# One more product summed into a PSUM bank, attention's first batch moved ahead of the weights, and products started while weights are still split

## The chip, the cores and the metric

One Trainium2 chip, one of its cores. The metric is the device time of one execution in microseconds (us); the median of three runs counts. A change of 0.2% of it is about 3 us.

## The reference, cut to what matters

```python
def _attn_ref(q, k, v, g_norm):              # q, k, v: (8, 8, 576, 64)
    kv = np.einsum('bhsd,bhse->bhde', k, v)
    out = np.einsum('bhsd,bhde->bhse', q, kv)
    rms = np.sqrt(np.mean(out * out, axis=-1, keepdims=True) + 1e-06)
    return (out / rms * g_norm).astype(np.float32)
...
x = attn_out.transpose(0, 2, 1, 3).reshape(4608, 512)
h = x @ w_in;   g = np.maximum(0.01 * h, h);  x = g @ w_out      # 512 -> 2048 -> 512
h = x @ w2_in;  g = h - np.tanh(h);           out = g @ w2_out   # 512 -> 2048 -> 512
```

The matrices have 4608 rows; the weights come as 8-byte floating point and are turned into 4-byte numbers on the chip.

## The kernel before, in words

Four matrix multiplications follow each other: "up 1" (512 to 2048, eight superblocks of 576 rows), "down 1" (2048 to 512), "up 2" (nine superblocks of 512 rows) and "down 2". Each is done with Winograd's form of Strassen's scheme: operands are cut in 2 by 2 blocks, sums of blocks (S on the left, T on the right) are formed, and seven products P1 to P7 are summed into four result blocks "11", "21", "12", "22". Every operand is kept as a high and a low 16-bit part, so that a product over one 128-deep slice is three matmuls (`three`, L490).

In up 1 and up 2 a unit of work is one of eight 128-column strips i of one superblock: seven products of six matmuls each. The matmuls of P1, P6 and P7 add up in one PSUM bank "a"; after each of these, ScalarE copies the running sum out (`keep`, L526 and L528), as c1, u2 and u3. P2 has bank "b", P4 bank "d", P5 and then P3 bank "c". VectorE adds such a bank to one of the copies (`add`, L537), which gives a result block in `g`: "11" from P2 and c1, "21" from u3 minus P4, "22" from P5 and u3, "12" from P3 on top of P5 and u2. A product that goes on in a bank waits until the copy or add before it has read the bank. TensorE's order inside a round is the table `ORDER`, with a lag in units. When "12" is there, ScalarE applies the activation (up 1, L1004) or ScalarE, VectorE and GpSimd do (up 2, L1151 and L1154), and the unit goes to DRAM.

Nothing is scheduled by the compiler: the class `Plan` keeps planned times for ScalarE ("A"), VectorE ("V") and GpSimd ("G") and one running time for TensorE (`plan.pe`), and emits every instruction in the order of its planned time. On the chip each engine takes its instructions in that order and waits at each for what it needs. `fit` looks for the first gap on an engine in which a job fits, and lets it overlap the next job by `OVER`.

The opening. q, k, v of batch 0 come in four pairs of heads (`load_pair`), between the weights of up 1, which come in 16 units of 512 KB (`convert`, n = 0): 3 units behind each of the four pairs, then the last 4. A unit is turned into 4-byte numbers by one ScalarE and four VectorE instructions (L315 to L338). After all 16 a scale is worked out (L254 to L269), and then `split_first` writes the high and low parts of the strips: ScalarE (L363) and VectorE (L366) each for three and four blocks, and GpSimd forms four differences (L373) in between. Attention (`pair`: pk, pq, po, pm) of a pair is some 36 fp32 matmuls with ScalarE copies between them; a batch's end is `norms`: a root, three reciprocals, a trip through DRAM (iv, bc), a GpSimd multiplication (xg, L879), four GpSimd sums (L469) and the high and low parts (L430, L437). Batch 1's four pairs are planned ahead of START, the planned time of the first product; the pairs of batches 2 to 7 are slipped between products of up 1 (`between1`). SyncE issues every DMA.

While up 1 runs, the weights of down 1 and then of up 2 are converted and split with the same instructions; those of down 2 during up 2.

Of the kernel before, what the change touches and what calls it, by code (L numbers as in the profile page):

```python
# [17 lines left out]
DRAM = bass.MemoryType.DRAM  # L18

# [9 lines left out]
NOP = 7  # L29
P = 128  # L30
# [13 lines left out]
class Plan:  # L44
# [5 lines left out]
    HAND, OVER = 0.25, 0.35  # L50
# [27 lines left out]
    def chain(self, t, steps):  # L78
# [3 lines left out]
        def go(k, t):  # L82
# [4 lines left out]
            for eng, dur, fn in some:  # L87
                t_ = t if eng is None else self.fit(eng, t, dur, min(self.OVER, dur / 3))
# [42 lines left out]
def body(ctx, tc, q, k, v, g_norm, w1, w2, w3, w4, out):  # L131
# [13 lines left out]
    NL, NM, NX = 22, 11, 8  # L145
# [149 lines left out]
    def convert(n, i, kk, t, land, keep=None):  # L295
# [50 lines left out]
        def store():  # L346
# [4 lines left out]
        steps = [(None, land, load), ("A", 0.7, one), ("V", 0.78, two), ("V", 0.45, shift), ("V", 0.7, low),  # L351
                 ("V", 0.7, high)]
        plan.chain(t, steps + ([(None, 0.0, store)] if keep is None else []))

    def right_stages(w, dst, scale):
# [15 lines left out]
        def less(o, a, b):  # L371
# [7 lines left out]
            ("G", 0.5, lambda: less(t2, b22, t1)), ("G", 0.5, lambda: less(t4, t2, b21)),  # L379
# [3 lines left out]
    def split_late(n, i, kk, t, place):  # L383

        held = {}

        def load():
            need(("wf", n, i, kk))
            need(f"s_w{n + 1}")
            held["u"] = place.take([P, NU], F32, "unit")  # L390
            nc.sync.dma_start(out=held["u"].ap, in_=wf[n, i, kk])
# [4 lines left out]
        def store():  # L396
            done_.add(("wd", n, i, kk))
            nc.sync.dma_start(out=wd[n, i][:, kk], in_=held["o"].ap.rearrange("p a b c -> p (a b c)"))
            place.give(held["u"])
# [3 lines left out]
        stages = right_stages(lambda: held["u"].ap, lambda: held["o"].ap, lambda: small[f"s_{name}"])  # L403
# [94 lines left out]
    class Blocks:  # L498

        def __init__(self, banks, width, place, scale=None, minus=None, ready=None):
            self.banks, self.n, self.place, self.ready = banks, width, place, ready
            self.scale = scale
            self.minus = -scale if isinstance(scale, float) else minus
            self.t, self.ps, self.done = {}, {}, set()
# [4 lines left out]
        def bank(self, p):  # L511
            which = BANK_OF[p]
            need = {6: "c1", 7: "u2", 3: "22"}.get(p)
            assert need is None or need in self.done, ("planned too late", plan.now, need)
            if p in (1, 2, 4, 5):
                self.ps[which] = bank(self.banks[which], f"ps_{which}")
            return self.ps[which][:, :self.n], p in (1, 2, 4, 5)

        def keep(self, nm):
            self.done.add(nm)  # L520
            self.t[nm] = X.take([P, self.n], F32, nm)
            src, t = self.ps["a"][:, :self.n], self.t[nm].ap
# [6 lines left out]
            if nm == "u3":  # L529
# [21 lines left out]
        def after(self, p, e):  # L551

            t, f = e + 0.15, self.n / 1000.0
            if p == 4:
                return e
            if p in (1, 6, 7):
                name = {1: "c1", 6: "u2", 7: "u3"}[p]
                end = plan.do("A", t, f + 0.15, lambda: self.keep(name))
                if p == 7:
                    self.u3 = end + 0.2  # L560
                    plan.do("V", self.u3, 1.2 * f + 0.14, lambda: self.add("21", "d", "u3", sub=True))
                return end
            blk, which, name = {2: ("11", "b", "c1"), 5: ("22", "c", "u3"), 3: ("12", "c", "u2")}[p]
            if p == 5:
                t = max(t, self.u3)
            return plan.do("V", t, 1.2 * f + 0.14, lambda: self.add(blk, which, name, last=True))

        u3 = 0.0
# [5 lines left out]

# [675 lines left out]
```

## Time and profile before

| | |
|---|---|
| median of 3 runs | 1580.79 us (1579.94 to 1581.8) |
| the profiled execution, its own time | 1581.95 us |
| its span in the profile | 1580.1 us |
| TensorE matmul busy | 1468.2 us (93%) |
| VectorE, ScalarE, GpSimd busy | 1311.1 us (83%), 864.4 us (55%), 749.4 us (47%) |
| mean granted TensorE clock | 0.972 |

The span runs from the first to the last instruction in the trace; 1.85 us of the execution lie around it. Matmuls are pipelined, so a busy TensorE may be one that goes on slowly. ps_a to ps_d are the banks of the products, PE is TensorE, DVE VectorE, ACT ScalarE, POOL GpSimd and SP SyncE. The granted clock 1.00 is 2.4 GHz, 0.50 is 1.2 GHz.

### The profile page before, as it was taken

What the parts mean: (1) busy time and instruction counts of PE and PEld (TensorE: products, weight loads), DVE (VectorE), ACT (ScalarE), POOL (GpSimd) and SP (SyncE); (2) the same over time, 40 slices, a digit from 0 to 9 for tenths busy, and PEclk for the clock granted to TensorE, in tenths of its full rate; (3) what the DMA queues carried; (4) which work ended last, traced back from release to release, by engine and by line L of the source; (5) the groups of instructions that cost most, each with busy time, mean ns of one, the idle gap of its engine ahead of it and who ended that gap; (6) DMA issues with size and microseconds to landing.
All of it is one profiled execution on the core that took longest, in us unless ns stands there. A gap on an engine that the chain in (4) does not pass through costs nothing. (4 is left out here: it accounts for less than half of the span.)

```text
span 1580.1 us, 33070 instructions
## 1 busy us (share of the span) xinstructions
PE 1468.2 (93%) x12658; PEld 1197.5 (76%) x12658; DVE 1311.1 (83%) x2113; ACT 864.4 (55%) x1381; POOL 749.4 (47%) x758
## 2 busy tenths in 40 slices
PE   5289998999899999999999899999999999999998
PEld 3157776766677777777777688878888888888887
DVE  5876777868777899899997799998999998888881
ACT  3367665656665745454453366656776655445450
POOL 0375311334533446667664244446886654444440
PEclk7589999999999999999999999999999999999999
DMA  9636887889966954555554855645668844444431
GB/s 223 193 96 182 268 272 245 267 267 298 296 248 216 375 197 162 176 171 192 168 180 153 295 194 194 210 158 197 222 244 311 306 126 144 136 138 151 139 120 34
DMA packets 190527, 322.59 MB, mean 204 GB/s; under 512 B 55712, under 2 KB 133024, under 8 KB 190368
## 3 DMA queue, kind: packets, MB, share of 16 engines
q1 hardware_dynamic: 190368, 320.48, 61.7%
q8 instruction: 99, 1.62, 0.4%
q14 instruction: 60, 0.49, 0.1%
HBM read 190.84 MB, written 129.56 MB: 203 GB/s over the span
## 5 line engine op out<-in xcount | busy, mean ns | idle before, releaser
L490 PEld LDWEIGHTS <-w 128*128 128x128 f16 x8400 | 819.4, 98 | 234.8 <-issue 58.3
L469 POOL TENSOR_TENSOR gl<-gl 128x256 f32<-128x256 f32 (+1 forms) x272 | 308.2, 1135 | 302.6 <-DVE gl L469 86.1
L490 PE MATMUL ps_c<-ops,w 128*128 128x288 f16 (+1 forms) x2400 | 331.7, 282 | 27.0 <-DVE g L537 26.8
L490 PE MATMUL ps_a<-ops,w 128*128 128x288 f16 (+1 forms) x2400 | 331.8, 283 | 7.5 <-ACT u L524 3.1
L373 POOL TENSOR_TENSOR unit<-unit 128x128 f32<-128x128 f32 x192 | 136.5, 715 | 109.3 <-DVE wo L366 78.0
L490 PEld LDWEIGHTS <-ops 128*128 128x128 f16 x1728 | 169.0, 98 | 24.9 <-issue 5.4
L490 PE MATMUL ps_b<-opa,w 128*128 128x288 f16 (+1 forms) x1200 | 174.7, 283 | 0.0
L490 PE MATMUL ps_d<-opa,w 128*128 128x288 f16 (+1 forms) x1200 | 173.0, 281 | 0.6 <-DVE g L537 0.5
L490 PE MATMUL ps_a<-opa,w 128*128 128x288 f16 (+1 forms) x1200 | 166.3, 282 | 5.2 <-DVE opa L437 2.6
L469 DVE TENSOR_TENSOR gl<-gl 128x256 f32<-128x256 f32 (+1 forms) x272 | 161.9, 601 | 3.7
L432 ACT ACTIVATE ops<-gl,inv 128x1024 f16<-128x1024 f32 x72 | 82.5, 1146 | 133.9 <-POOL gl L469 133.9
L1154 POOL TENSOR_TENSOR g<-g,th 128x512 f32<-128x512 f32 x72 | 101.1, 1406 | 95.9 <-ACT th L1151 95.3
L879 POOL TENSOR_TENSOR xg<-xg,bc 128x1152 f32<-128x1152 f32 x16 | 42.8, 2681 | 206.1 <-DMA bc<-iv 135.6
L490 PEld LDWEIGHTS <-opa 128*128 128x128 f16 x1296 | 127.6, 99 | 15.6 <-DVE opa L439 0.2
L439 DVE SCALAR_TENSOR_TENSOR ops<-gl,inv,ops 128x1024 f16<-128x1024 f32 x72 | 105.7, 1469 | 31.3 <-ACT ops L432 31.3
L430 ACT ACTIVATE ops<-gl 128x1152 f16<-128x1152 f32 x64 | 74.2, 1161 | 94.8 <-POOL gl L469 94.8
L437 DVE TENSOR_TENSOR ops<-gl,ops 128x1152 f16<-128x1152 f32 x64 | 97.9, 1530 | 7.4 <-ACT ops L430 7.2
L490 PE MATMUL ps_a<-w,ops 128*128 128x256 f16 x864 | 97.2, 273 | 3.4 <-ACT u L528 2.8
L490 PE MATMUL ps_c<-w,ops 128*128 128x256 f16 x864 | 97.3, 273 | 0.2 <-DVE osb L537 0.2
L528 ACT ACTIVATE u<-ps_a,up 128x256 f32<-128x256 f32 x144 | 68.2, 473 | 49.2 <-PE ps_a L490 43.8
L469 POOL TENSOR_TENSOR x1g<-x1g 128x256 f32<-128x256 f32 x72 | 65.7, 916 | 53.9 <-DVE opa L439 25.0
L537 DVE SCALAR_TENSOR_TENSOR g<-ps_c,u 128x288 f32<-128x288 f32 x128 | 57.7, 451 | 39.2 <-PE ps_c L490 39.1
(118 smaller groups left out, 2203.6 us busy)
## 6 DMA issues: line engine op xcount, KB each, us to landing
g<-g SPq DMA_DIRECT2D x64, 576.0 KB, 4.9
gl<-g SPq DMA_DIRECT2D x64, 576.0 KB, 4.9
g<-g SPq DMA_DIRECT2D x72, 512.0 KB, 3.3
gl<-g SPq DMA_DIRECT2D x72, 512.0 KB, 4.5
wd<-wo SPq DMA_DIRECT2D x48, 448.0 KB, 3.3
w<-wd SPq DMA_DIRECT2D x24, 896.0 KB, 6.9
words<-in_moe_w_in_dram SPq DMA_DIRECT2D x64, 256.0 KB, 5.2
words<-in_moe_w_out_dram SPq DMA_DIRECT2D x64, 256.0 KB, 4.3
```

Source lines behind the costliest of these rows:

```text
L373: nc.gpsimd.tensor_tensor(out=o, in0=a, in1=b, op=ALU.subtract)
L430: nc.scalar.activation(out=o, in_=i_, func=AF.Copy)
L432: nc.scalar.activation(out=o, in_=i_, func=AF.Identity, scale=scale())
L437: nc.vector.tensor_tensor(out=o, in0=i_, in1=h, op=ALU.subtract)
L439: nc.vector.scalar_tensor_tensor(out=o, in0=i_, scalar=scale(), in1=h, op0=ALU.mult, op1=ALU.subtract)
L469: lambda: e.tensor_tensor(out=g()[:, o], in0=g()[:, a], in1=g()[:, b], op=op),
L490: nc.tensor.matmul(out=out_, lhsT=a, rhs=c, start=start and m == 0, stop=stop and m == n - 1, skip_group_check=not fresh,)
L528: nc.scalar.activation(out=t, in_=src, func=AF.Identity, scale=self.scale)
L537: nc.vector.scalar_tensor_tensor(out=o, in0=src, scalar=self.minus if sub else self.scale, in1=t, op0=ALU.mult, op1=ALU.add,)
L879: nc.gpsimd.tensor_tensor(out=x, in0=x, in1=held[kk].ap, op=ALU.mult)
L1154: e.tensor_tensor(out=g()[:, n], in0=g()[:, n], in1=held["t"].ap[:, n], op=ALU.subtract)
```

## The change

Four things are changed, three of them in the two up stages' scheduling.

- P4 in up 1 and up 2: the right-hand sum T4 is formed with the other sign (`minus4`, for the weights n = 0 and 2), and P4 adds up in bank "a" behind P1, P6 and P7. ScalarE copies the sum straight into `g` as block "21". Bank "d" is not used there; bank "a" is taken from three banks in turn. The VectorE add of "21" is not issued. The order within a round is new (`ORDER1`, `ORDER2`); in up 2 P3 runs two units behind instead of one.
- The opening: one weight unit behind each of batch 0's pairs instead of three, then the other 12. The copies of po into xg for batch 0 go from VectorE to ScalarE. START is `last + 45` instead of `last + 58`. Three of batch 1's pairs are planned ahead of START, the fourth five products behind it; batches 2 and 3 begin later.
- The splits of up 1's strips are planned 4.2 us apart instead of 5.0, and may run three strips ahead of the buffers instead of two.
- The plan's costs: ScalarE jobs may overlap by 0.6 (0.35 before), all by half of their length (a third before); conversion jobs are planned somewhat differently. One slot more in pool M, one less in L; up 2's units for splitting come from M.

The diff, with unchanged lines cut:

```diff
@@ -47,7 +48,7 @@
-    HAND, OVER = 0.25, 0.35
+    HAND, OVER = 0.25, {"A": 0.6, "V": 0.35, "G": 0.35}
     def __init__(self):
@@ -85,7 +86,7 @@
-                t_ = t if eng is None else self.fit(eng, t, dur, min(self.OVER, dur / 3))
+                t_ = t if eng is None else self.fit(eng, t, dur, min(self.OVER[eng], dur / 2))
                 def run(fn=fn):
@@ -142,7 +143,7 @@
-    NL, NM, NX = 22, 11, 8
+    NL, NM, NX = 21, 12, 8
@@ -348,11 +349,12 @@
-        steps = [(None, land, load), ("A", 0.7, one), ("V", 0.78, two), ("V", 0.45, shift), ("V", 0.7, low),
-                 ("V", 0.7, high)]
+        slow = 1.0 if keep else 1.1
+        steps = [(None, land, load), ("A", 0.7, one), ("V", 0.72 * slow, two), ("V", 0.4 * slow, shift),
+                 ("V", 0.63 * slow, low), ("V", 0.63 * slow, high)]
-    def right_stages(w, dst, scale):
+    def right_stages(w, dst, scale, minus4):
@@ -376,18 +378,20 @@
-            ("G", 0.5, lambda: less(t2, b22, t1)), ("G", 0.5, lambda: less(t4, t2, b21)),
+            ("G", 0.5, lambda: less(t2, b22, t1)),
+            ("G", 0.5, (lambda: less(t4, b21, t2)) if minus4 else (lambda: less(t4, t2, b21))),
-    def split_late(n, i, kk, t, place):
+    def split_late(n, i, kk, t, place, place_u=None):
+        place_u = place_u or place
         def load():
-            held["u"] = place.take([P, NU], F32, "unit")
+            held["u"] = place_u.take([P, NU], F32, "unit")
         def room():
@@ -396,11 +400,11 @@
         def store():
-            place.give(held["u"])
+            place_u.give(held["u"])
-        stages = right_stages(lambda: held["u"].ap, lambda: held["o"].ap, lambda: small[f"s_{name}"])
+        stages = right_stages(lambda: held["u"].ap, lambda: held["o"].ap, lambda: small[f"s_{name}"], n == 2)
@@ -499,34 +503,41 @@
         def __init__(self, banks, width, place, scale=None, minus=None, ready=None):
+            self.one4 = "d" not in banks
-            self.t, self.ps, self.done = {}, {}, set()
+            self.t, self.ps, self.done, self.kept = {}, {}, set(), {}
         def scaled(self, scale, minus):
         def bank(self, p):
-            which = BANK_OF[p]
-            need = {6: "c1", 7: "u2", 3: "22"}.get(p)
+            which = "a" if p == 4 and self.one4 else BANK_OF[p]
+            need = {6: "c1", 7: "u2", 3: "22", 4: "u3" if self.one4 else None}.get(p)
-            if p in (1, 2, 4, 5):
+            start = p in (1, 2, 5) or p == 4 and not self.one4
+            if start:
-            return self.ps[which][:, :self.n], p in (1, 2, 4, 5)
+            return self.ps[which][:, :self.n], start
         def keep(self, nm):
-            self.t[nm] = X.take([P, self.n], F32, nm)
-            src, t = self.ps["a"][:, :self.n], self.t[nm].ap
+            if nm == "21":
+                t = self.place(nm)
+            else:
+                self.t[nm] = X.take([P, self.n], F32, nm)
+                t = self.t[nm].ap
+            src = self.ps["a"][:, :self.n]
-            if nm == "u3":
+            if nm == ("21" if self.one4 else "u3"):
         def add(self, blk, which, nm, sub=False, last=False):
@@ -551,30 +562,24 @@
         def after(self, p, e):
-            if p == 4:
+            if p == 4 and not self.one4:
-            if p in (1, 6, 7):
-                name = {1: "c1", 6: "u2", 7: "u3"}[p]
+            if p in (1, 6, 7, 4):
+                name = {1: "c1", 6: "u2", 7: "u3", 4: "21"}[p]
-                if p == 7:
-                    self.u3 = end + 0.2
-                    plan.do("V", self.u3, 1.2 * f + 0.14, lambda: self.add("21", "d", "u3", sub=True))
+                self.kept[name] = end + 0.2
+                if p == 7 and not self.one4:
+                    plan.do("V", self.kept[name], 1.2 * f + 0.14, lambda: self.add("21", "d", "u3", sub=True))
-            if p == 5:
-                t = max(t, self.u3)
+            t = max(t, self.kept[name])
-        u3 = 0.0
     def mm(T):
-    ORDER = ((2, 0), (6, 0), (4, 0), (3, 1), (1, -1), (7, 0), (5, 0))
-    def up(blk, T, NS, xops, act, scale, banks, between, freed):
+    def up(blk, T, NS, xops, act, scale, banks, order, between, freed):
@@ -618,17 +620,24 @@
-        for n in range(-1, N + 1):
-            for p, lag in ORDER:
+        def place(m):
+            def get(b):
+                if m not in g:
+                    g[m] = L.take([P, 4, T], F32, "g")
+                return g[m].ap[:, BLOCKS.index(b)]
+            return get
+        for n in range(-1, N + 2):
+            for p, lag in order:
-                if n == N:
-                    plan.pe += 1.4
-                if n == 0 and p in (6, 7):
+                if m == 0 and p in (6, 7) or m == N - 1 and p == 4:
+                if blk == 0 and m < NP and p == 1:
+                    plan.pe += SLOW
-                    bk[m] = Blocks(banks(m), T, None, None if callable(scale) else scale)
+                    bk[m] = Blocks(banks(m), T, place(m), None if callable(scale) else scale)
@@ -818,11 +827,18 @@
             def copy():
-                nc.vector.tensor_copy(out=xg[b, kk].ap[:, 2 * n + r], in_=po[r][:, :T1])
+                o_ = xg[b, kk].ap[:, 2 * n + r]
+                if b == 0:
+                    nc.scalar.activation(out=o_, in_=po[r][:, :T1], func=AF.Copy)
+                else:
+                    nc.vector.tensor_copy(out=o_, in_=po[r][:, :T1])
-            plan.do("V", end, 0.46, copy)
+            if b == 0:
+                plan.do("A", end, 0.42, copy)
+            else:
+                plan.do("V", end, 0.46, copy)
         def m():
@@ -905,8 +921,8 @@
     def place_w1(i, kk):
         def get():
-                if i < NP - 2:
-                    kept[i] = Held(wpool.tile([P, 2 * NU], F32, tag=f"w{i + 2}", name=f"w1f{i}"), None)
+                if i < NP - 3:
+                    kept[i] = Held(wpool.tile([P, 2 * NU], F32, tag=f"w{i + 3}", name=f"w1f{i}"), None)
@@ -917,8 +933,8 @@
-        order += [("w",) + u for u in UNITS[3 * hp:3 * hp + 3]]
-    order += [("w",) + u for u in UNITS[12:]]
+        order += [("w",) + u for u in UNITS[hp:hp + 1]]
+    order += [("w",) + u for u in UNITS[4:]]
@@ -932,11 +948,11 @@
     def split_first(i, kk):
-            lambda: kept[i].ap[:, NU * kk:NU * kk + NU], lambda: wt[i][:, kk], lambda: small["s1g"]
+            lambda: kept[i].ap[:, NU * kk:NU * kk + NU], lambda: wt[i][:, kk], lambda: small["s1g"], True
-        elif i >= NP - 2:
+        elif i >= NP - 3:
@@ -947,8 +963,8 @@
-            what = ("w", 0, i - 2, 1) if i >= 2 else "s_w1"
-            when(what, plan.now + 0.3 + 5.0 * i, lambda i=i: pair_(i))
+            what = ("w", 0, i - 3, 1) if i >= 3 else "s_w1"
+            when(what, plan.now + 0.3 + 4.2 * i, lambda i=i: pair_(i))
@@ -965,23 +981,24 @@
-    START = last + 58.0
+    START = last + 45.0
+    FIRST = {1: (-18.0, -11.5, -5.0, 5), 2: (20, 32, 43, 54), 3: (67, 78, 89, 100)}
-            n0 = NOP * (NP * b - 16 + 2 * hp)
-            pos[b, PAIRS[hp]] = n0
+            pos[b, PAIRS[hp]] = FIRST[b][hp] if b in FIRST else NOP * (NP * b - 16 + 2 * hp)
-            t_ = max(last, START - 14.0 + 1.45 * n0 / NOP)
-            at(min(t_ - 8.0, t_), lambda b=b, c=c, held=held: load_pair(b, c, held))
+            t_ = max(last, START + n0)
+            at(t_ - 8.0, lambda b=b, c=c, held=held: load_pair(b, c, held))
@@ -1004,12 +1021,15 @@
     def banks1(n):
-        return dict(a=n % 2, b=2, c=3, d=4)
+        return dict(a=(0, 1, 4)[n % 3], b=2, c=3)
+    SLOW = 0.4
+    ORDER1 = ((1, 0), (7, 1), (5, 1), (2, 0), (6, 0), (4, 1), (3, 1))
     def freed_to(n):
-    up(0, T1, NS1, x0ops, leaky, H1_SCALE, banks1, between1, freed_to(1))
+    up(0, T1, NS1, x0ops, leaky, H1_SCALE, banks1, ORDER1, between1, freed_to(1))
@@ -1140,7 +1160,7 @@
-    spread(lambda i, kk, t: split_late(2, i, kk, t, L), UNITS, end1 + 45.0, end2 - 28.0)
+    spread(lambda i, kk, t: split_late(2, i, kk, t, L, M), UNITS, end1 + 45.0, end2 - 28.0)
     def tanh(g, s):
@@ -1160,14 +1180,16 @@
     def banks2(n):
-        return dict(a=n % 2, b=(2, 5)[n % 2], c=(3, 6)[n % 2], d=(4, 7)[n % 2])
+        return dict(a=(0, 1, 4)[n % 3], b=(2, 5)[n % 2], c=(3, 6)[n % 2])
+    ORDER2 = ((1, 0), (7, 1), (5, 1), (3, 2), (6, 0), (4, 1), (2, 0))
     def between2(n):
-    up(1, T2, NS2, x1ops, tanh, lambda s: consts[s][1:3], banks2, between2, freed_to(3))
+    up(1, T2, NS2, x1ops, tanh, lambda s: consts[s][1:3], banks2, ORDER2, between2, freed_to(3))
```

## Rows read from the trace of the kernel before

**Rows 1.** Busy time by stage: opening, up 1, down 1, up 2.
```profile
0.00:101.64 101.64, 49.12 (x303) 28.08 (x304) 68.57 (x139) 41.72 (x86) 32.13 (x48) 0.66 0.71 183
101.64:534.13 432.49, 412.42 (x3594) 310.50 (x3592) 322.14 (x628) 272.72 (x524) 160.79 (x180) 0.99 0.79 256
534.13:878.51 344.38, 335.30 (x2711) 265.62 (x2709) 310.66 (x435) 162.61 (x210) 201.07 (x188) 1.00 0.55 188
878.51:1238.85 360.34, 337.82 (x3032) 296.91 (x3030) 334.41 (x574) 235.06 (x377) 210.62 (x210) 0.99 0.64 228
```

The columns are the stretch and its length, then busy us (instructions) of PE, PEld, DVE, ACT and POOL, the granted clock, the share of the DMA engines and GB/s.

**Rows 2.** Timeline of the opening, all engines: start, length, instruction, and the wait before.
```profile
35.01 10.84 SPq L303 DMA_DIRECT2D words<-in_moe_w_in_dram  x14
...
60.29 1.27 DVE L338 SCALAR_TENSOR_TENSOR w1f<-words,w1f 128x512 int32<-128x512 int32 x2
...
64.28 2.61 POOL L879 TENSOR_TENSOR xg<-xg,bc 128x1152 f32<-128x1152 f32 x1 [62.97 <-DVE r_w L235]
...
64.53 2.38 DVE L269 TENSOR_TENSOR s1g<-s_w,gcol 128x1 f32<-128x1 f32 x1
...
66.94 0.61 ACT L363 ACTIVATE w<-w1f,s1g 128x384 f16<-128x384 f32 x1 [15.06 <-DVE s1g L269]
...
78.07 1.33 ACT L363 ACTIVATE w<-w1f,s1g 128x512 f16<-128x512 f32 x2 [5.43 <-POOL w1f L373]
...
101.64 0.90 PE L490 MATMUL ps_a<-opa,w 128*128 128x288 f16 x6
```

**Rows 3.** Timeline of TensorE behind the first products, attention's pieces among them.
```profile
107.16 0.41 PE L794 MATMUL pq<-ident,q 96*128 96x96 f32 x3
107.41 0.90 PE L490 MATMUL ps_a<-ops,w 128*128 128x288 f16 x6
108.14 0.90 PE L490 MATMUL ps_c<-ops,w 128*128 128x288 f16 x6
...
110.60 0.65 PE L810 MATMUL po<-qt,kvd 128*128 128x288 f32 x2
...
115.34 0.68 PE L832 MATMUL pm<-sq,sel 128*32 128x288 f32 x4
...
117.53 0.92 PE L774 MATMUL pk<-v,k 96*64 96x64 f32 x24
```

**Rows 4.** Groups by line and shape: count, busy us, mean ns, idle before.
```profile
L528 ACT ACTIVATE u<-ps_a,up 128x256 f32<-128x256 f32 x144 | 68.2, 473 | 49.2 <-PE ps_a L490 43.8 <-DMA x<-xst 5.0 <-DVE inv L1079 0.2
...
L373 POOL TENSOR_TENSOR w1f<-w1f 128x128 f32<-128x128 f32 x64 | 39.3, 640 | 10.3 <-DVE w L366 9.9
...
L537 DVE SCALAR_TENSOR_TENSOR g<-ps_d,down,u 128x256 f32<-128x256 f32 x72 | 34.3, 477 | 16.2 <-ACT u L528 16.2
...
L537 DVE SCALAR_TENSOR_TENSOR g<-ps_d,u 128x288 f32<-128x288 f32 x64 | 29.1, 454 | 25.1 <-ACT u L526 24.7
```

**Rows 5.** Who TensorE waited for in up 1: us, times, longest.
```profile
PE ps_c L490 <- DVE g L537: 9.5, 8, 2.2
PE po L810 <- ACT qt L802: 5.8, 2, 4.0
...
PE ps_a L490 <- ACT c L526: 1.7, 2, 1.3
```

**Rows 6.** The same for up 2, and VectorE's first wait there.
```profile
PE ps_c L490 <- DVE g L537: 16.7, 24, 2.2
PE ps_a L490 <- ACT u L528: 2.5, 1, 2.5
...
DVE g L537 <- ACT u L528: 16.2, 25, 1.4
```

**Rows 7.** Timeline around 234 us: GpSimd and VectorE side by side.
```profile
233.48 2.68 POOL L879 TENSOR_TENSOR xg<-xg,bc 128x1152 f32<-128x1152 f32 x1 [1.26 <-DMA bc<-iv]
233.95 2.76 DVE L332 SCALAR_TENSOR_TENSOR unit<-words,unit 128x512 int32<-128x512 int32 x1
...
340.79 0.69 DVE L332 SCALAR_TENSOR_TENSOR unit<-words,unit 128x512 int32<-128x512 int32 x1
```

More of the change, by code (lines that the diff above doesn't have):

```diff
@@ L588, in product @@
                 need(("w", 2 * blk, i, kk))
-            if p == 2:
-                g[n] = L.take([P, 4, T], F32, "g")
-                bk[n].place = lambda b: g[n].ap[:, BLOCKS.index(b)]
             o, start = bk[n].bank(p)
@@ L607, in store @@
                 nc.sync.dma_start(out=gd[blk, s, i], in_=g[n].ap.rearrange("p o t -> p (o t)"))
-                L.give(g[n])
+                L.give(g.pop(n))
                 del bk[n]
```

## The prediction

> **What bounds the kernel now.** First the busy time by stage [rows 1], to see where TensorE isn't fed. In the opening, 101.64 us long, it is busy for 49.1, at a mean clock of 0.66 of 2.4 GHz. In up 1 its clock is 0.99. A product of six matmuls takes 108.14 - 107.41 = 0.73 us there, while its row says 0.90 [rows 3]: the last 0.17 of each row lie under the next product, so a wait that is listed costs 0.17 more than its number. 64 units x 7 products x 0.735 = 329 us of the 432.5 of up 1; attention's pieces fill most of the rest. In up 2 the product has 256 columns for 288: 0.655 us, and 72 x 7 x 0.655 = 330 of 360.3 us [rows 1]. There 30 us are lost, and nothing but products runs. So two places have room: the opening, and up 2.
>
> Next the timeline of the opening, to see what its end hangs on [rows 2]. SyncE has issued the last words by 45.9 us; VectorE ends the conversions at 61.6, because they piled up. The scale then takes until 66.9 (L269 alone 2.38 us, while GpSimd is at xg for 2.61). GpSimd is at batch 0's xg and sums and at the weights' differences at once, ScalarE waits for it (5.43 us at 78), and the first product starts at 101.64, 2.4 us behind the plan: the old plan puts batch 0's pairs 8.9 us apart (3.2 for a pair, 3 x 1.9 for units), the last at 34.2, its end 7 later, and START 58 behind that, at 99.2.
>
> Last the lists of waits [rows 5, 6]. In up 2 TensorE waits 24 times, 16.7 us, for VectorE to have read bank c; with the 0.17 each it is 20.8 us of the 30 lost. VectorE itself waits there 25 times, 16.2 us, for ScalarE's u: the groups show that all of it stands ahead of the add of block "21" [rows 4]. So that add sits at VectorE's head until u3 is there, and "22", which frees bank c for P3, sits behind it. In up 1 there are 8 such waits of 9.5 us together, and 5.8 us for attention's qt.
>
> **The change, part by part.**
>
> *P4 in bank a.* It removes 64 adds of 454 ns and 72 of 477 from VectorE, 63.4 us, and gives ScalarE as many copies: 72 x 0.473 = 34.1 us in up 2 [rows 4] and in up 1 64 of about as much, 30 at most. Busy time of itself sets nothing: in up 2 VectorE falls from 334 to 300 of some 345 us, ScalarE rises from 235 to 269 [rows 1], and neither is full. What counts is the wait at c. "22" no longer stands behind "21", which is 0.47 us sooner, and up 2's P3 comes a whole round (some 4.6 us) later. The mean wait is 16.7 / 24 = 0.70 us, the longest 2.2 [rows 6], so both are covered. The gain in up 2 is at most 20.8 us. What is late next is bank a: P6, P7 and now P4 wait for ScalarE's copy, each with three products between, 1.97 us. A copy needs 0.17 + 0.47; it holds unless ScalarE is over 1.3 us behind. Before, 144 such waits cost 2.5 us in one place [rows 6]; with 216 and a fuller ScalarE I put 4 us. Up 2: 20.8 less some 10% that stays, less 4 and rounded down for the extra round: 15 gained, bounds 8 and 21.
>
> In up 1 P3 still runs three products behind P5 and has one bank c, so only the 0.47 us of "21" and a less crowded VectorE help: of the 9.5 + 8 x 0.17 = 10.9 us [rows 5] I take half, 5. ScalarE there is busy 273 of 432 us [rows 1]; its waits on a cost 1.7 us in two places, which could triple. Bounds 0 and 10. The 5.8 us for qt come from ScalarE standing behind late xg; that isn't touched.
>
> *The opening.* Pairs 5.1 us apart on the queue (3.2 + 1.9), but 7.0 long on TensorE: planned at 7.5, 14.5, 21.5 and 28.5, end 35.5, START 80.5. That is 18.7 us earlier by plan. What the chip allows: all words still have to come, 45.9 us of issues, since the bytes are the same. VectorE is rid of eight xg copies (ScalarE, which takes them, is busy 41.7 of 101.6 us). By the plan's lines four units are through early and the fifth lands at 26.9; 12 units with four jobs each, L338's being 0.64, are some 29 us, and the three reciprocals 2: done at about 58. But batch 0's xg, 2.61 us twice, and eight sums now fall on GpSimd while VectorE still converts, where before they began at 64.28, behind it [rows 2]. What that costs is in the trace: L332 takes 2.76 us beside an xg of 2.68, and 0.69 alone [rows 7]. Two xg: about 2 x 2.1 = 4 us. So conversions end at 62, the scale near 66, a gain of about 1 where the plan counts on 4. The first strip then needs ScalarE and VectorE, eight differences of 0.64 [rows 4] and both again, some 9 us: 75. The three pairs that run ahead need copies by ScalarE, whose queue waits for the scale, and take three times 6.5 to 7: 66 + 20 = 86. I take the first product at 85.5: 16 us gained.
>
> The Trainium skill, page "SBUF — State Buffer", section "Who interferes with whom", has the rule for these rows: GpSimd and a VectorE instruction with two inputs in SBUF share a port pair, and whoever has it holds the other up for its whole instruction. The trace agrees (2.76 us against 0.69). By the rule alone the eight sums would block too, and the opening's term would be some 4 us smaller than mine.
>
> Against the 16 stands batch 1's fourth pair, now among the products: .92 + 2 x .41 + 2 x .65 + .68 = 3.7 us by its rows [rows 3], less 0.16 for each of six groups that run under their neighbours, about 3. And there are the products among the splits: 64 differences x 0.64 = 41 us of GpSimd [rows 4], a strip each 5.1 us where the plan says 4.2, so ScalarE's splits stand 0.9 us more behind with each strip, 6 by the eighth, and the copies that free bank a stand behind them. Attention between products (a pair of 3 us to about 11 products) stretches a unit from 5.1 to some 7 us, which gives part of it back; I put 4 us. The opening: 16 - 3 - 4 = 9, bounds 0 (all of START's gain waited for later) and 15.
>
> *The rest* (slots, overlaps, sizes in the plan) changes no instruction. It shifts which job goes first; the down stages, where one such chance wait may come or go, I put at 0, bounds -4 and +4. The split units of up 2 in another pool, and bank d freed, cost nothing: they're places, with no transfer more.
>
> Sum: 9 + 5 + 15 = 29 us. The profiled execution took 1581.95 (span 1580.1 and 1.85 around it), 1.2 above the median: 1553 by the one, 1552 by the other. I say 1552.
>
> **The rivals.**
>
> *The opening gives nothing.* The products start early but stand until GpSimd has split the strips, and end the first superblock when they did before. For it: the contention [rows 7], 5.43 us of ScalarE waiting for GpSimd already before [rows 2]. Against it: a unit with attention in it takes longer (7 us) than a strip (5.1). Then 0 + 5 + 15: 1561.
>
> *Up 2's waits stay.* VectorE is at 93% there, and its many other jobs, not block "21", may be what holds bank c. For it: waits of up to 2.2 us [rows 6], longer than one add. Against it: P3's extra round is 4.6 us. Then the removed work alone gives some 4: 9 + 5 + 4, 1563.
>
> *Bank a becomes the bound (slower).* Four copies per unit in one chain, each between two products. If each of 136 units waits 0.3 us for u3, that is 41 us against 29: 1593. It decides from 29 / 136 = 0.21 us a unit. For it: ScalarE, allowed to overlap by 0.6, is given jobs closer together. Against it: before, three waits in 136 units cost 4.2 us in all [rows 5, 6].
>
> *No change:* the first two together, 1572, with half of the third's price, about 1580.
>
> **How the numbers follow.** Forecast 0.58; opening gives nothing 0.17; up 2's waits stay 0.12; no change 0.05; slower 0.08. The forecast's own range is 1542 to 1561 (bounds of its terms taken as independent). Most of the chance lies on one side, so the range for 8 in 10 goes from the upper bounds of the larger terms, 15 + 5 + 21 + 4 = 45 (1536 by the median), to the two middle rivals, 1561 and 1563, with up 1's 5 us missing as well and rounded up (1570). About 3 us, 0.2%, can be told from no change: faster 0.88, same 0.04, slower 0.08.
>
> **What would show it.** Right: the first ps_a of a product near 85 us; up 2 some 345 us long with less than 4 us of ps_c waiting for VectorE; no ps_d in the up stages; ps_a's waits for ScalarE 3 to 8 us in both up stages; the conversions' last L338 near 62 with an L332 or L338 over 1.5 us beside xg. Wrong: a row of ps_a waits of 0.2 us and more behind ScalarE's u3 in every unit; TensorE's busy time between 85 and 125 no more than before in that stretch; or a half clock among the first products, which costs as long again as it lasts.

## The result, and the profile after

The changed kernel takes 1553.77 us (median of 4 runs, 1551.36 to 1555.7) where the kernel before takes 1581.19 (4 runs). The ratio is 0.983 [0.9816, 0.9845]: 1.7% faster, 1.8 us from the forecast and inside its range. The profiled execution took 1555.7 us, its span is 1553.9.

Busy time by stage of the changed kernel, cut where its stages begin (opening, up 1, down 1, up 2, down 2; columns as in rows 1):

```profile
0.00:86.46 86.46, 38.58 (x265) 21.15 (x266) 56.89 (x122) 37.39 (x81) 28.53 (x35) 0.75 0.76 204
86.46:525.17 438.71, 417.56 (x3650) 313.61 (x3648) 308.71 (x581) 303.20 (x606) 165.47 (x194) 0.99 0.81 257
525.17:864.93 339.76, 331.59 (x2692) 262.99 (x2691) 305.26 (x433) 157.02 (x204) 196.77 (x186) 1.00 0.55 188
864.93:1213.18 348.25, 336.13 (x3030) 297.98 (x3031) 303.84 (x500) 262.62 (x451) 221.78 (x210) 0.99 0.66 235
1213.18:1553.90 340.72, 333.53 (x3026) 296.62 (x3023) 270.92 (x338) 150.35 (x185) 142.73 (x134) 0.99 0.43 136
```

Before, the first unit of down 1 started at 537.11, not where [rows 1] cut it; with that cut the stages of the kernel before are these:

```profile
101.64:537.11 435.47, 414.78 (x3611) 312.25 (x3610) 324.61 (x633) 274.96 (x527) 162.43 (x181) 0.99 0.80 256
537.11:878.51 341.40, 332.94 (x2693) 263.86 (x2691) 308.20 (x431) 160.37 (x207) 199.43 (x186) 1.00 0.55 187
```

Stage by stage the span of 1580.1 lost 26.2 us: the opening 101.64 - 86.46 = 15.2, up 1 435.5 - 438.7 = -3.2, down 1 1.6, up 2 360.3 - 348.25 = 12.1, down 2 0.6. The same lengths (us) for every kernel of this study, each from its one profiled execution:

| kernel | opening | up 1 | down 1 | up 2 | down 2 |
|---|---|---|---|---|---|
| before | 101.6 | 435.5 | 341.4 | 360.3 | 341.3 |
| changed | 86.5 | 438.7 | 339.8 | 348.3 | 340.7 |
| x1, P4 alone | 101.8 | 434.0 | 339.3 | 348.6 | 340.6 |
| x2, opening alone | 86.8 | 441.1 | 338.5 | 361.6 | 339.3 |
| x3, P3 one behind in up 2 | 85.3 | 433.4 | 340.5 | 349.5 | 337.5 |
| x4, xg planned later | 85.1 | 427.6 | 339.4 | 348.3 | 340.7 |
| x5, ten X slots | 85.1 | 435.3 | 338.9 | 342.6 | 340.9 |
| x6, scale first | 87.1 | 439.1 | 338.7 | 348.3 | 341.1 |
| x7, before, xg later | 99.5 | 427.2 | 343.9 | 362.4 | 341.2 |
| x8, x4 to x6 together | 88.2 | 428.5 | 339.8 | 340.6 | 340.8 |
| x9, four sums on VectorE | 86.2 | 442.3 | 338.2 | 349.4 | 340.8 |
| x10, x6 and x9 | 89.2 | 441.1 | 340.5 | 348.8 | 340.7 |
| x11, x4 and x5 | 86.4 | 425.2 | 338.4 | 343.8 | 340.6 |
| x12, pairs planned earlier | 82.6 | 442.3 | 340.1 | 348.4 | 340.1 |

Kernels in which no edit touches up 1 differ there by up to 9 us (x3 and x9), in down 1 by 5.7 (x7 and x9) and in down 2 by 3.8 (x3 and before); so one profile bears a statement on a stage only where its lists of waits bear it too.

Who TensorE waited for in up 1 and, below the line of dots, in up 2 of the changed kernel (us, times, longest; before: [rows 5] and [rows 6]):

```profile
PE ps_c L494 <- DVE g L548: 12.2, 13, 4.2
PE ps_a L494 <- ACT u L537: 4.0, 3, 3.1
PE ps_a L494 <- ACT c L537: 2.8, 1, 2.8
...
PE ps_a L494 <- ACT u L539: 6.9, 2, 6.8
PE ps_c L494 <- DVE g L548: 2.4, 2, 1.8
```

In up 2 bank c's 24 waits have gone but for two. What stands instead is mainly a single wait at bank a, 6.8 us long. In up 1 bank c is waited for no less than before. [rows 5] end 3 us early; with up 1 taken up to 537.11 the kernel before has 10.1 us there, for 12.2 now:

```profile
PE ps_c L490 <- DVE g L537: 10.1, 9, 2.2
```

The opening, from the timeline of the changed kernel (start, length, instruction, wait before it; [rows 2] answer to it):

```profile
55.79 8.67 POOL L895 TENSOR_TENSOR xg<-xg,bc 128x1152 f32<-128x1152 f32 x2 [54.49 <-DMA bc<-iv]
57.53 1.88 DVE L339 SCALAR_TENSOR_TENSOR w1f<-words,w1f 128x512 int32<-128x512 int32 x3
61.92 0.92 ACT L434 ACTIVATE opa<-xg 128x864 f16<-128x864 f32 x1 [15.35 <-POOL xg L895]
62.87 1.90 DVE L441 TENSOR_TENSOR opa<-xg,opa 128x288 f16<-128x288 f32 x1 [3.46 <-ACT opa L434]
64.69 0.15 DVE L255 TENSOR_REDUCE m_w<-mw 128x1 f32<-128x16 f32 x1
...
69.79 0.61 ACT L365 ACTIVATE w<-w1f,s1g 128x384 f16<-128x384 f32 x1 [0.83 <-DVE s1g L270]
...
82.32 1.23 ACT L365 ACTIVATE w<-w1f,s1g 128x512 f16<-128x512 f32 x2 [1.72 <-POOL w1f L375]
83.45 0.44 ACT L794 ACTIVATE kvd<-pk 64x64 f32<-64x64 f32 x2
83.95 0.47 PE L803 MATMUL pq<-ident,q 96*128 96x96 f32 x3 [2.44 <-ACT kvd L794]
...
86.46 1.56 PE L494 MATMUL ps_a<-opa,w 128*128 128x288 f16 x6
```

The conversions end at 57.53 + 1.88 = 59.4. GpSimd's two xg took 8.67 us; alone one takes 2.61. VectorE then stood at an xg subtraction (L441) that waited 3.46 us for ScalarE, ahead of the column maxima, and the scale was used at 69.79: 2.9 us later than before (66.94), not sooner. The first product came at 86.46 all the same. The rows ahead of it show the last link: the third pair's `kvd` on ScalarE, behind splits that wait for GpSimd's differences. The product's row is 1.56 us long, not 0.90, and the next one starts 1.40 us behind it, not 0.735: from 84.4 to 87.8 the granted clock was 0.50.

### The profile page after: what moved, and what is told of

It is laid out like the page before. It is cut to its first block, busy times and chain, and to the rows that moved or that the text cites. A ratio compares the mean times of both kernels' runs of the same rounds, so it can differ in the third digit from the quotient of the medians.

```text
span 1553.9 us, 33173 instructions
## 1 busy us (share of the span) xinstructions
PE 1457.4 (94%) x12658; PEld 1192.3 (77%) x12658; DVE 1245.6 (80%) x1969; ACT 910.6 (59%) x1525; POOL 755.3 (49%) x758
## 5 line engine op out<-in xcount | busy, mean ns | idle before, releaser
L494 PE MATMUL ps_c<-ops,w 128*128 128x288 f16 (+1 forms) x2400 | 319.5, 282 | 14.8 <-DVE g L548 14.5
L494 PE MATMUL ps_a<-opa,w 128*128 128x288 f16 (+1 forms) x2016 | 284.0, 282 | 11.2 <-ACT u L539 6.8
L375 POOL TENSOR_TENSOR unit<-unit 128x128 f32<-128x128 f32 x192 | 130.1, 679 | 103.4 <-DVE wo L368 75.0
L1174 POOL TENSOR_TENSOR g<-g,th 128x512 f32<-128x512 f32 x72 | 112.7, 1565 | 95.4 <-ACT th L1171 92.2
L895 POOL TENSOR_TENSOR xg<-xg,bc 128x1152 f32<-128x1152 f32 x16 | 46.5, 2909 | 202.7 <-DMA bc<-iv 202.7
L441 DVE TENSOR_TENSOR ops<-gl,ops 128x1152 f16<-128x1152 f32 x64 | 97.8, 1527 | 16.7 <-ACT ops L434 16.6
L443 DVE SCALAR_TENSOR_TENSOR opa<-gl,inv,opa 128x768 f16<-128x768 f32 x72 | 89.7, 1246 | 0.0
L365 ACT ACTIVATE wo<-unit,s_w 128x384 f16<-128x384 f32 (+1 forms) x96 | 63.1, 663 | 40.6 <-POOL unit L375 37.1
```

The costliest lines, as they stand in the source:

```text
L365: nc.scalar.activation(out=dst()[:, 0, a:b], in_=cols(0, n), func=AF.Identity, scale=scale())
L375: nc.gpsimd.tensor_tensor(out=o, in0=a, in1=b, op=ALU.subtract)
L441: nc.vector.tensor_tensor(out=o, in0=i_, in1=h, op=ALU.subtract)
L443: nc.vector.scalar_tensor_tensor(out=o, in0=i_, scalar=scale(), in1=h, op0=ALU.mult, op1=ALU.subtract)
L494: nc.tensor.matmul(out=out_, lhsT=a, rhs=c, start=start and m == 0, stop=stop and m == n - 1, skip_group_check=not fresh,)
L895: nc.gpsimd.tensor_tensor(out=x, in0=x, in1=held[kk].ap, op=ALU.mult)
```

## The experiments

Each was timed against the kernel before; its median in the four groups of runs was 1582.55 (x1 to x4), 1580.71 (x5 to x8), 1578.15 (x9 to x11) and 1580.3 (x12).

### x1 and x2: each half alone

x1 is the changed kernel with the opening of before: the conversions' order, pools, copies and splits of before, and (its core; P4, the new orders and the plan's costs stay)

```
-    START = last + 45.0
+    START = last + 58.0
...
-            pos[b, PAIRS[hp]] = FIRST[b][hp] if b in FIRST else NOP * (NP * b - 16 + 2 * hp)
+            pos[b, PAIRS[hp]] = NOP * (NP * b - 16 + 2 * hp)
```

x2 has the new opening and the plan's costs and, for both up stages, the old order, bank d and the old signs (its core):

```
-    ORDER2 = ((1, 0), (7, 1), (5, 1), (3, 2), (6, 0), (4, 1), (2, 0))
+    ORDER2 = ((2, 0), (6, 0), (4, 0), (3, 1), (1, -1), (7, 0), (5, 0))
```

> The changed kernel with the old opening (three weight units behind each pair, START at last + 58, all four pairs of batch 1 ahead of it, splits 5.0 us apart, xg copies on VectorE); P4 in bank a, the new orders and the plan's costs stay. If the parts add up (my theory): up 2 about 350 us long as in the changed kernel, TensorE's waits for VectorE at bank c there under 4 us, up 1 no shorter than before, so 10 to 15 us faster than before, 1566 to 1571. If up 2's gain hangs on the opening (other chance meetings of jobs): up 2 back at 360 and no more than 3 us gained.

> The changed kernel with P4 as before: bank d, the VectorE add of block 21, T4's old sign, the old order in both up stages. If the parts add up: first product near 86 us, up 2 again 358 to 362 us with 15 us or more of waits at bank c, so 11 to 15 us faster than before, 1566 to 1570. If products among the splits need ScalarE's copies of the new scheme to go on: more than 4 us of waits of products between 86 and 130 us and under 8 us gained.

x1 took 1566.33 us, ratio 0.9914 [0.9887, 0.9941]; x2 1567.43, 0.9922 [0.9892, 0.9951]. Against 1582.55 they gain 16.2 and 15.1, together 31 where the whole change gains 27.4 against its own runs of before: within their intervals (0.0027 and 0.003 of 1582 is 4 to 5 us each) the halves add up. Both keep the plan's costs and the sizes of the pools, so what these are worth is counted twice; no run has them alone. By stages P4 alone gives 1.5 us in up 1 and 11.7 in up 2. The opening alone gives 14.8 at the first product, and up 1 takes 5.6 of it back: TensorE is busy there for 419.13 us, 4.35 more than before, and stands for 1.3 more. In x2's up 2 (TensorE's waits) the old picture is back:

```profile
PE ps_c L494 <- DVE g L548: 17.4, 25, 2.8
PE ps_a L494 <- ACT u L539: 2.1, 1, 2.1
```

### x3: P3 one unit behind in up 2 instead of two

```
-    ORDER2 = ((1, 0), (7, 1), (5, 1), (3, 2), (6, 0), (4, 1), (2, 0))
+    ORDER2 = ORDER1
```

> The changed kernel, with up 2 in up 1's order: P3 one unit behind, three products after P5, instead of two units behind; P4 stays in bank a. If the add of block 21 at VectorE's head was what held bank c (my theory): waits of ps_c for VectorE in up 2 stay under 6 us and the time within 4 us of the changed kernel's 1554. If P3's extra round is what does it: the waits come back to 12 us and more and the time is 10 to 16 us longer, 1564 to 1570.

1549.92 us, 0.9821 [0.9784, 0.9858]. Up 2 is 349.5 long, 1.2 more than in the changed kernel. The whole is 3.9 us shorter; in the profile that lies in up 1 and down 2, which the edit doesn't touch. TensorE's waits in up 2:

```profile
PE ps_c L494 <- DVE g L548: 5.2, 9, 1.3
PE ps_a L494 <- ACT u L539: 4.4, 2, 2.8
```

So of the 17.4 us (x2), 12.2 go when block "21"'s add does, with P3 three products behind P5 in both kernels, and 2.8 more with P3's extra round. VectorE's queue shows the same: its waits for ScalarE's u in up 2 are 17.6 us in 20 places in x2 and stand no more in x3's list. The queue was the cause, the round a small help.

### x4: xg of batches 1 to 7 planned later

```
-            more.append([(None, 6.0, lambda kk=kk: load(kk)), ("G", 2.7, lambda kk=kk: scale(kk))] + stages)
+            more.append([(None, 10.0 if b else 6.0, lambda kk=kk: load(kk)), ("G", 2.7, lambda kk=kk: scale(kk))] + stages)
```

The plan expects `bc` 10 instead of 6 after its issue, so that xg and what reads it stand further back on all queues. `if b` is true for every batch but 0, so the edit acts on batches 1 to 7, in x7, x8 and x11 too, where the expectations say 1 to 3. No work is less. What it aims at is to be seen in the changed kernel's up 1. GpSimd, ScalarE and TensorE:

```profile
184.25 2.62 POOL L895 TENSOR_TENSOR xg<-xg,bc 128x1152 f32<-128x1152 f32 x1 [8.11 <-DMA bc<-iv]
186.90 0.92 ACT L434 ACTIVATE opa<-xg 128x864 f16<-128x864 f32 x1 [6.68 <-POOL xg L895]
188.74 0.41 ACT L537 ACTIVATE u<-ps_a 128x288 f32<-128x288 f32 x1
189.21 0.90 PE L494 MATMUL ps_a<-ops,w 128*128 128x288 f16 x6 [3.10 <-ACT u L537]
192.64 1.60 PE L494 MATMUL ps_c<-ops,w 128*128 128x288 f16 x6 [2.29 <-DVE g L548]
```

`bc` comes late, xg 8.11 us after GpSimd was free for it; ScalarE stands 6.68 us at xg's split while the copy that frees bank a is queued behind, and TensorE stands. Then it is slow as well: from 190.2 to 197.0 the granted clock was 0.50, and the product at 192.64 took 1.60 us, where the one before had taken 0.90.

> The changed kernel with the multiplication of xg planned 10 us instead of 6 us behind the loads of bc for batches 1 to 7, so that ScalarE's and VectorE's jobs on xg stand further back in their queues. If up 1's waits (bank c 12.2 us, bank a 6.8 us) come from ScalarE and VectorE standing behind a late xg (my theory now): these waits fall by half or more, and the time by 6 to 12 us, 1542 to 1548. If they come from VectorE's load itself: no change within 3 us.

1543.32 us, 0.977 [0.9742, 0.9798]: 10.4 less than the changed kernel. Up 1 is 427.6, 11.1 less, all other stages within 1.4. Between 120 and 190 us ScalarE waits 1.10 + 1.78 us for GpSimd's xg, where in the changed kernel it waits 15.2 in five places. In all of up 1 its split of a freshly scaled xg waits 1.8 us once, for 23.5 in 8 places (18.2 in 8 before). TensorE's waits in up 1:

```profile
PE ps_c L494 <- DVE g L548: 7.1, 5, 2.7
PE ps_a L494 <- ACT u L537: 4.5, 4, 2.6
```

The waits at the two banks fell from 19.0 us to 11.6, by less than the half that was expected. The rest of the 11.1 is TensorE's busy time, 413.67 us for 417.56 with the same products: behind the first of them, its up 1 has 3.4 us at the granted clock 0.50, the changed kernel's 10.2. So late xg was some 40% of these waits and part of the slow stretches; what holds the other waits isn't shown.

### x5: ten X slots

```
-    NL, NM, NX = 21, 12, 8
+    NL, NM, NX = 21, 12, 10
```

The long wait in up 2 of the changed kernel. SyncE, then ScalarE and TensorE:

```profile
862.90 4.55 SPq L420 DMA_DIRECT2D w<-wd  x4
867.54 2.44 SPq L1064 DMA_DIRECT2D x<-xst  x2
...
882.17 0.47 ACT L539 ACTIVATE u<-ps_a,up 128x256 f32<-128x256 f32 x1 [8.33 <-DMA x<-xst]
...
882.70 1.44 PE L494 MATMUL ps_a<-opa,w 128*128 128x256 f16 x6 [6.75 <-ACT u L539]
```

ScalarE's `u` takes a slot of X whose last content, a result tile of down 1, is still being stored: the store is issued behind four strips of 896 KB and has landed at 882, 14 us later. TensorE waits 6.75 us for that `u`, and the three products behind it start 1.23 to 1.28 us apart, not 0.655: the granted clock was 0.50 from 879.7 to 886.5.

> Ten X slots instead of eight. Theory: the one wait of 6.75 us in the changed kernel's up 2 (TensorE at bank a, behind ScalarE's u, which stands 8.33 us for a slot whose last content, a result tile of down 1, is still being stored) comes from the slots' number: with two more the wait falls under 3 us and up 2 goes from 348.3 to 343 to 346 us, the other stages stay within 2 us: 1549 to 1552. Rival A: what is late is the transfer itself and any number of slots is in use when down 1 ends: the wait stays at 6 to 7 us and up 2 at 348. Rival B: it is the price of P4's fourth copy in bank a: the same, no change.

1547.09 us (1543.94 to 1551.11), 0.9804 [0.9773, 0.9835]. Time and stage lie just below what was expected; up 1, which should have stayed, is 3.4 us shorter too, within what it varies. Up 2 is 342.6, 5.7 less, and TensorE's waits there:

```profile
PE ps_a L494 <- ACT c L539: 3.2, 2, 2.7
PE ps_c L494 <- DVE g L548: 2.4, 2, 1.7
...
PE ps_a L494 <- ACT u L539: 0.2, 1, 0.2
```

Two more slots take TensorE's wait away, with P4's copy in place. The kernel before had it too (ScalarE 5.0 us at `x<-xst`, [rows 4]). But its size goes with P4's half of the change: ScalarE stands 8.4 us there in x1, 4.7 in x2 and 3.0 in x3, which differs from the changed kernel in up 2's order alone. How the order sets it isn't shown.

### x6, x9, x10 and x12: what sets the first product

x6 plans the first scale 4 us sooner, x9 gives GpSimd's first two sums of each xg of batch 0 to VectorE, x10 does both, x12 plans batch 1's three early pairs 6 us sooner:

```
-                weight_scale(n, plan.now + 1.0)
+                weight_scale(n, plan.now + (-3.0 if n == 0 else 1.0))
...
                 lambda kk=kk: xg[b, kk].ap, x0ops[b][kk], None, T1, done=lambda kk=kk: L.give(xg[b, kk]), pieces=2,
+                first=nc.vector if b == 0 else None,
...
-    FIRST = {1: (-18.0, -11.5, -5.0, 5), 2: (20, 32, 43, 54), 3: (67, 78, 89, 100)}
+    FIRST = {1: (-24.0, -17.5, -11.0, 5), 2: (20, 32, 43, 54), 3: (67, 78, 89, 100)}
```

> The steps of the first weights' scale are planned 4 us sooner, so that on VectorE all of them stand ahead of the four subtractions of batch 0's xg (before them in the changed kernel: one of 1.90 us that itself waits 3.46 us for ScalarE ahead of the column maxima, and three more ahead of the last step). Theory: VectorE standing behind those subtractions is what puts the scale at 69.8 us although the conversions end at 59.4; with it ahead the scale is there at 64 to 65.5 and the first product comes 2 to 4 us sooner than 86.46, at 82.5 to 84.5; total 1550 to 1552. Rival: ScalarE's copies of the three pairs that run ahead and their subtractions set the first product, and they are later by what the scale is sooner: first product 86 to 87, total within 2 us of 1553.8.

> Four of the eight sums of batch 0's xg go from GpSimd to VectorE. Theory: the first product waits for the third pair's copies on ScalarE, which stand there behind splits that wait for GpSimd (1.19, 1.72 and 0.83 us in the changed kernel), and GpSimd is late because sums and differences both fall on it from 66 us on; 4 x 0.79 us less on it bring the first product 2 to 4 us sooner than 86.46, to 82.5 to 84.5, though the scale comes at 70 as before. Rival: the third pair's place on ScalarE's queue sets it, whatever GpSimd does: 85.5 to 87.

> The four sums on VectorE and the scale's steps ahead of the subtractions, both edits together. Theory (GpSimd and the scale are both links of the way to the first product, and either alone uncovers the other): the first product at 80 to 83 us. Rival: neither is on that way: 85.5 to 87.

> Batch 1's three pairs that run ahead of the products are planned 6 us sooner, START stays; on ScalarE's queue the third pair's kvd then stands behind three splits of the weights' strips in place of eight. Theory (the first product is set by where the third pair's copies stand on ScalarE's queue, since each split there waits for GpSimd's differences): first product at 78 to 83 in place of 86.46; total 1548 to 1552, if the first strips feed the products that come sooner. Rival A: the first product moves but the products then wait for the strips, which GpSimd splits no sooner: first product under 83, waits of 2 us and more among the first products, total within 2 us of 1553.8. Rival B: it stays at 85.5 or later, because the scale or the subtractions set it.

| kernel | scale used | first product | time, ratio |
|---|---|---|---|
| changed | 69.8 | 86.5 | 1553.77, 0.983 [0.9816, 0.9845] |
| x6 | 66.4 | 87.1 | 1555.55, 0.9852 [0.9831, 0.9872] |
| x9 | 70.1 | 86.2 | 1554.27, 0.9847 [0.9817, 0.9878] |
| x10 | 66.3 | 89.2 | 1557.84, 0.9871 [0.9843, 0.9899] |
| x12 | 71.6 | 82.6 | 1556.75, 0.9855 [0.9839, 0.9872] |

Two theories fell. A scale that is 3.4 us sooner brings nothing (x6, x10), nor does GpSimd with four sums less (x9). In each of them the third pair's `kvd` stays behind a split that waits for GpSimd: of xg in x6 (2.41 us), of the weights in x9 (1.29) and x10. In x10 that wait is longest, and its first product lies outside what both its theory (80 to 83) and its rival (85.5 to 87) gave. Its ScalarE:

```profile
85.05 1.23 ACT L365 ACTIVATE w<-w1f,s1g 128x512 f16<-128x512 f32 x2 [3.42 <-POOL w1f L375]
86.18 0.43 ACT L794 ACTIVATE kvd<-pk 64x64 f32<-64x64 f32 x2
```

x12 moves that `kvd` on the queue itself, and the first product comes at 82.6 though the scale comes latest of all. So the place on ScalarE's queue sets it. But the total doesn't gain. The first three products of x12, TensorE:

```profile
82.62 0.91 PE L494 MATMUL ps_a<-opa,w 128*128 128x288 f16 x6
83.36 0.90 PE L494 MATMUL ps_b<-opa,w 128*128 128x288 f16 x6
91.27 1.60 PE L494 MATMUL ps_a<-ops,w 128*128 128x288 f16 x6 [7.00 <-ACT c L537]
```

After two products it waits 7 us for ScalarE's copy `c`, which stands behind splits that wait for GpSimd (2.28 and 1.73 us there), and the product behind takes 1.60 us for 0.90; the granted clock from 86 to 110 us is 0.86, for 0.96 in the changed kernel. That was this run's rival A, but for a total 3 us above the changed kernel's where it gave 2. An earlier first product alone gives nothing, then. That GpSimd's differences bound what the opening can still give is an inference: no run here makes them faster.

### x7: the same edit to xg in the kernel before

> The kernel before, with xg of batches 1 to 3 planned 10 instead of 6 after its load. Theory: ScalarE and VectorE standing behind a late xg are a loss that up 1 had all along (5.8 us at qt, 10.1 at bank c before) and that the change neither made nor removed: up 1 goes from 435.5 to 426 to 430 us and the total falls by 6 to 10 us, to 1571 to 1575. Rival: in the kernel before bank c's waits have VectorE's many adds for their reason, and only the changed kernel's denser opening makes late xg costly: up 1 gains under 3 us, the total 1578 or more.

1570.69 us (10 runs), 0.9943 [0.9928, 0.9958] against its 1580.71: 10.0 us. Up 1 is 427.2, 8.3 less, and bank c waits 5.5 us for 10.1; the 5.8 us at `qt` [rows 5] are gone from its list, and so are ScalarE's 18.2 us for a freshly scaled xg. ScalarE and VectorE standing behind a late xg is a loss that was there all along, which the change neither removed nor made much larger.

### x8 and x11: the edits together

x11 is the changed kernel with the edits of x4 and x5, x8 has that of x6 as well.

> The changed kernel with all three edits: xg of batches 1 to 3 planned 10 after its load, ten X slots, the first scale ahead of the subtractions. Theory: they act at three places (up 1, the start of up 2, the opening) and add up: 10.5 + 3 + 3, so 1536 to 1539 us. Rival: the opening's gain is waited for again in up 1 and the slots' in up 2, and what is left is that of the planned xg alone: 1542 to 1545.

> xg of batches 1 to 3 planned 10 after its load and ten X slots, without the edit to the scale. If the two add up: 10.5 + 5.6 by their stages, up 1 at 427 to 430 us and up 2 at 341 to 344, total 1537 to 1541. Rival: a time above 1543 with those two stages as short says that something else gives it back, in the down stages; with up 1 above 433 that the planned xg's gain was chance.

x8: 1547.34 us (1539.74 to 1550.03), 0.9791 [0.9759, 0.9823]. x11: 1540.08 (1536.42 to 1543.69), 0.9762 [0.9731, 0.9794]. x11's stages are as short as x4's and x5's (425.2 and 343.8), so these two add up; it is the fastest kernel here, 38 us under its 1578.15 of before. x8 was expected at 1536 to 1539. Its profiled execution (1539.74) was near that, its median was not; with the scale first the opening is 1.8 us longer (88.2 for 86.4). Why its executions spread over 10 us, where x4's lie within 1.7, stays open.

## Why the prediction was right

By its own steps, with gains in us; the parts are measured in the run named, the sum is that of the whole change, and so they differ by 0.8:

| step | said | measured |
|---|---|---|
| first product | 16 | 15.2 |
| batch 1's fourth pair, products among splits | -3 and -4 | -5.6 together (x2) |
| up 1, bank c | 5 | 1.5 (x1) |
| up 2 | 15 | 12.1 |
| rest | 0 ± 4 | 2.2 |
| sum | 29 | 26.2 (spans) |

*The opening.* The time of the first product was right, the way to it was not, and that is luck. It said that conversions end at 62 because VectorE is held up beside GpSimd's xg. They ended at 59.4, and GpSimd was held up; the scale then came at 69.8 instead of 66, because VectorE stood at the subtractions. The third pair's place on ScalarE's queue covered both errors (x6, x9, x12), so the working from the scale ("66 + 20") gave a good number by a chain that x6 refutes: with the scale at 66.4 the first product is at 87.1. The eight sums, which it also put beside the conversions, began at 66.24 us, 6.8 behind the last of them.

*Among the splits.* Of products waiting there, for which it put 4 us, between 86.46 and 125 us there is one wait of 0.67. TensorE is busy for 37.87 of those 38.54 us, for 34.15 before. The 5.6 us that up 1 took back in x2 are some 3 for the pair (by its rows), some 1.4 for the first two products, which took 1.65 us for 0.90, and 1.3 of waits. Half a clock among the first products was one of the prediction's signs of being wrong. It came, in the changed kernel for one product; there it cost 1.40 - 0.735 = 0.67 us: about half of the 1.40 that it lasted, not as long again.

*Up 1.* This is the term that failed: "half of the 10.9 us of waits at bank c" for P4's add being gone. The waits at c did not shrink in the changed kernel (12.2 for 10.1; with the same up 1, x3 has 9.3). In x1, with P4's add gone and the opening of before, they are 8.7 us, and up 1 as a whole is 1.5 shorter, no more than such a stage varies. In x4 and x7, where only xg's place in the plan changes, the waits at c fall by 5.1 and 4.6 us and up 1 by 11.1 and 8.3. The waits' releaser in the list was VectorE's add, but for up to half of them what stood ahead was a job on a late xg, which the prediction made answerable for `qt` alone and in which P4 has no part. The other half stays open.

*Up 2.* The waits at c fell from 16.7 us in 24 places to 2.4 in 2. With 0.17 for each of 22, that is 14.3 + 3.7 = 18.0; it said 20.8 less 10%, 18.7. Bank a took back 6.9 + 0.6 - 2.5 = 5.0; it said 4, but for a fuller ScalarE. Nearly all of it is one wait for an X slot (x5), a cause that the prediction didn't name; its 4 came close by luck. The four copies of a unit in one chain cost nothing that the lists show: none of the waits comes unit by unit. P3's extra round is a smaller part of it than P4's add (x3).

The rivals. *The opening gives nothing*: no, 9.2 of 14.8 stay (x2). *Up 2's waits stay*: no. *Bank a becomes the bound*: no; it is waited for 6.8 us in up 1 and 7.5 in up 2, as the prediction gave for right (3 to 8), not the 41 of the rival.

Four of the prediction's numbers don't come out as written. 20.8 less 10% less 4 is 14.7, which 15 rounds up, not down. Its terms' bounds, taken as independent, give 1541 to 1565, not 1542 to 1561. "No change" comes to 1592 with half of the third's 41 us; about 1580 needs half of the 12 by which they pass 29. Bank c's 9.5 us in up 1 are 10.1 when up 1 ends at 537.11. None of them moves the forecast by 1 us.

Of the port pair the Trainium skill, page "SBUF — State Buffer", section "Who interferes with whom", says that the instruction that has it keeps it to its end while the other blocks. The trace agrees, and shows what the prediction's reading of [rows 7] left out: who was there first. Here VectorE was, and it lost nothing. The conversions follow one another without a gap, and GpSimd's two xg, whose row starts at 55.79 among them, are done at 64.46: 59.41, where the conversions end, and 2 x 2.61 give 64.63. x12 has the other order: one conversion begins at 63.84, while the second xg runs (62.14 to 64.75), and takes 1.47 us for 0.68.

## What to carry to other kernels

A wait names the instruction that ended it; before a change is credited with removing it, follow that instruction's own queue to what stands ahead of it, here often a job on data that land later than the plan put them. In a kernel whose queues are written out in advance, a job planned a few us later can cost nothing and free every engine behind it (x4, x7: 8 to 11 us for one number), and a chain can't be shortened at a link that another queue covers (x6, x9), nor past the engine that feeds what follows (x12). When a slot's last use is a store, that store's place on the DMA queue is part of the slot's price (x5).

## What the runs showed that was not expected

In this opening VectorE's back-to-back conversions, with two inputs each, held GpSimd off until the last had ended, and then the smallest VectorE instruction paid. In x6 no subtraction of xg stands between conversions and column maxima, and its VectorE shows two instructions of one column each, 0.16 us elsewhere:

```profile
58.81 0.15 DVE L255 TENSOR_REDUCE m_w<-mw 128x1 f32<-128x16 f32 x1
58.99 0.15 DVE L257 TENSOR_SCALAR t_w<-m_w 128x1 int32<-128x1 int32 x1
59.18 2.18 DVE L260 SCALAR_TENSOR_TENSOR m_w<-m_w,t_w 128x1 int32<-128x1 int32 x1
61.40 2.54 DVE L264 TENSOR_TENSOR m_w<-m_w,gabs 128x1 f32<-128x1 f32 x1
```

Each takes nearly the length of one xg of GpSimd, 2.61 us alone (the two there run from 55.03 to 63.92), while the instructions with one input just before them keep their 0.15. In this kernel it hides, since the scale doesn't set the first product.
